# A decode block on one core: part of the query weights' load moves to ScalarE's DMA queue, ahead of x

## The chip, the cores and the metric

The kernel runs on one core of one Trainium2 chip. The metric is the device time of one execution in microseconds (us); smaller is better. The engines are called as in the profile: PE (TensorE), DVE (VectorE), ACT (ScalarE), POOL (GpSimd) and SP (SyncE). A transfer is issued by an engine on that engine's own DMA queue; SP's is q1 in the profile, ACT's is q10, and q8 carries the core's own fetches of instructions. All of them are served by the core's 16 DMA engines. Tile sizes are partitions x elements, all float32.

## The reference

One decoding step for two sequences of one token each: layer norm, attention over a cache of 8192 keys for 16 heads of 256, and a bilinear gated feed-forward layer.

```python
def _A_ref(x, k_cache, v_cache, wq, wo):        # B=2, Sq=1, D=448, H=16, Sk=8192, Dh=256
    q = (x @ wq).reshape(B, Sq, H, Dh).transpose(0, 2, 1, 3)
    scores = jnp.einsum("bhqd,bhkd->bhqk", q, k_cache) * (Dh ** -0.5)
    p = _softmax(scores, axis=-1)
    o = jnp.einsum("bhqk,bhkd->bhqd", p, v_cache)
    return o.transpose(0, 2, 1, 3).reshape(B, Sq, H * Dh) @ wo

x = A_x
h = x + _A_ref(_layernorm(x), A_k_cache, A_v_cache, A_wq, A_wo)
g, u = _layernorm(h) @ B_w_gate, _layernorm(h) @ B_w_up
return h + (g * u) @ B_w_down
```

The two caches are 2 x 16 x 8192 x 256 numbers each, 268 MB; the weights are small beside them (wq is 7.3 MB).

## The kernel before, in words

There are 32 pairs of head and sequence (NQ), numbered i. For each, the keys (128x16384, 64 KB in each of 128 partitions) come into one of two buffers `k0` and `k1`, the values (the same size) into the only buffer `v`. DVE makes the scores: it multiplies the keys by the query spread over the partitions (`qb`), L436, and sums over 256, L445, each in a piece of 16 columns of keys and one of 48. ACT makes the exponentials, PE the product with the values (L527).

The work of each engine is written out in one list for each engine (the class `Engine`), and an instruction carries the names of what it waits for; nothing is reordered by a planner. All large transfers are issued by SP, in the order of its list, each with `load` (L176 in the profile):

- `wq`, the query weights, packed as 128x14336. They are put into the value buffer `v`, as `wq_t`.
- the first 16 columns of keys of pair 0 (`k0`, 128x4096), the other 48 (128x12288), then the keys of pair 1 (128x16384). These wait for nothing.
- then, in turn, the keys of pair i+1, which wait for the largest score of pair i-1 (`m`, L458), and the values of pair i, which wait for PE's last product of pair i-1. The values of pair 0 wait for `all_q` instead: PE must have finished the whole projection of the query, since the values overwrite `wq_t`.

At the start, ACT issues the load of `x` (2x448, L259). From it DVE makes the centred x (L312 to L323), PE transposes it (L338), DVE copies it to `xz` (L345) and clears four accumulators in PSUM (L359, whose last one gives the name `set`). PE then waits for `wq`, `xz` and `set` together, and projects the query in eight rounds of 512 columns (L376): 64 matmuls, of which the first 16 give the query of pair 0, which ACT copies and PE and ACT spread to `qb` (L393 to L413). DVE's first score waits for that.

Of the kernel before, what the change touches and what calls it, by code (L numbers as in the profile page):

```python
# [8 lines left out]
B, D, H, SK, DH, F = 2, 448, 16, 8192, 256, 1792  # L9
EPS = 1e-5  # L10
P = 128
# [15 lines left out]
FF = [(n, g) for n in range(4) for g in range(4) if n < FG[g] // P]  # L27
DOWN = (4, 4, 2, 2, 1, 1)
NPART, OPEN_AFTER = 8, 9

LAYOUT = (
    (slice(0, P), slice(0, DC - 1), slice(0, DC - 1)),
# [121 lines left out]
def decode_block(nc, x, k_cache, v_cache, wq, wo, wg, wu, wd, out):  # L154
# [6 lines left out]
    def landing(name):  # L161
        return nc.alloc_semaphore(name=name)
# [4 lines left out]
    V, A, G, S, T = (  # L167
        Engine(nc, *engine)
        for engine in (
            (nc.vector, "dve"), (nc.scalar, "act", ("qsel", "qb"), ("q",)), (nc.gpsimd, "pool"),  # L170
            (nc.sync, "sp"), (nc.tensor, "pe", ("qp", "Q0"), ("heads",)),
        )
    )

    def load(line, dst, src, sem, name, *waits, n=16):
        line.do(lambda: line.e.dma_start(dst, src).then_inc(sem, 16), *waits)  # L176
        known[name] = sem, n
# [59 lines left out]
    wq_t = v_flat[:, : 3 * H * DH + H * DH // 2]  # L237
# [8 lines left out]
    def keys_of(cache, i, lo, hi):  # L246
        h, b = divmod(i, B)
        return cache[b, h].rearrange("(p j) d -> p j d", p=P)[:, lo:hi, :]
# [6 lines left out]
            n=16 * (i // 2 + 1),  # L255
        )

    s_x = landing("x")
    nc.scalar.dma_start(x_sb, x.rearrange("b s d -> (b s) d")).then_inc(s_x, 16)  # L259
    known["x"] = s_x, 16  # L260
    load(S, wq_t, wq, landing("wq"), "wq")
    load(S, k_sb[0][:, :HC], keys_of(k_cache, 0, 0, HC), landing("k0"), "k0")
    load_k(0, lo=HC)
    load_k(1)
# [618 lines left out]
```

## Time and profile before

| | |
|---|---|
| time, median of 3 runs | 1301.42 us (1301.16 to 1301.53) |
| profiled execution: its time, its span | 1300.94 us, 1299.6 us |
| HBM read | 561.19 MB |
| DVE busy | 1132.5 us, 87% of the span |
| PE busy | 471.1 us, 36% |
| DMA, mean busy share of the 16 engines, by queue q1 | 99.8% |
| wq: 7168 KB on SP's queue, from issue to landing | 19.7 us |

The span runs from the first to the last instruction. Windows and timelines count microseconds from the span's start. In the view of the DMA over a short window, the window is cut into 40 equal slices, and a packet (one row of a transfer, in one partition) is counted whole in the slice in which it starts, so a slice can show more than 100% or far more GB/s than the engines can move; such a view tells when rows start. Besides the rows, a queue's packets contain the small completion marks, one for each DMA engine that took part in a transfer.

### The profile page before, as it was taken

How to read it: one execution, taken by the hardware profiler on the slowest of the kernel's cores; microseconds unless marked ns; L12 is line 12 of the kernel's file. 1: busy time of each engine (PE TensorE's matmuls, PEld its weight loads, DVE VectorE, ACT ScalarE, POOL GpSimd, SP SyncE). 2: the span in 40 equal slices, each digit the busy share in tenths (PEclk: the TensorE clock that was granted, in tenths of full speed). 3: DMA queues.
4: the chain of work that ended last, by engine and by line, in shares of the span. 5: the costliest groups of instructions: out<-in, count | busy, mean ns of one | idle time of the engine just before them, and what ended most of it. 6: DMA issues, size and time to landing. Idle time of an engine off the chain costs nothing.

```text
span 1299.6 us, 7381 instructions
## 1 busy us (share of the span) xinstructions
PE 471.1 (36%) x2870; PEld 149.9 (12%) x2870; DVE 1132.5 (87%) x265; ACT 83.5 (6%) x245; POOL 0.8 (0%) x8
## 2 busy tenths in 40 slices
PE   3643214334323433323334322433322343332368
PEld 0111001101001101101101101101100110100113
DVE  1999988889888889888889988889988888988861
ACT  1100000000000000000000000000000000000000
POOL 0000000000000000000000000000000000000000
PEclk9866566666566666556666656666656666655669
DMA  9999999999999999999999999999999999999998
GB/s 412 428 450 422 448 424 444 426 436 436 422 450 422 450 422 448 424 444 426 436 436 422 450 422 450 422 448 424 444 426 436 436 422 450 422 450 422 448 422 365
DMA packets 11382, 561.28 MB, mean 432 GB/s; under 512 B 1394, under 2 KB 1652, under 8 KB 2420
## 3 DMA queue, kind: packets, MB, share of 16 engines
q1 hardware_dynamic: 11376, 561.25, 99.8%
q8 instruction: 2, 0.03, 0.0%
q10 hardware_dynamic: 4, 0.00, 0.0%
HBM read 561.19 MB, written 0.06 MB: 432 GB/s over the span
## 4 chain that ended last, share of the span: by engine, by line
DMA 48%; DVE 41%; issue 8%; PE 2%; SPq 0%; DVEq 0%; ACT 0%
DMA k<-in_A_k_cache_dram 45%; DVE s L445 21%; DVE k L436 19%; DMA v<-in_wq_dram 2%; DMA v<-in_wd_dram 1%; PE bank L376 1%; PE bank L561 1%; PE bank L527 1%; DVE m L458 0%; DVE nm L464 0%; DVE rl L469 0%; SPq L176 0%; PE bank L551 0%; DVEq L149 0%; PE bank L367 0%
## 5 line engine op out<-in xcount | busy, mean ns | idle before, releaser
L436 DVE TENSOR_TENSOR k<-k,qb 128x4096 f32<-128x4096 f32 x64 | 555.3, 8676 | 122.6 <-DMA k<-in_A_k_cache_dram 98.9
L445 DVE TENSOR_REDUCE s<-k 128x16 f32<-128x4096 f32 x64 | 555.2, 8675 | 1.1
L527 PE MATMUL bank<-v,p 128*2 128x512 f32 x2048 | 289.5, 729 | 348.0 <-DMA v<-in_A_v_cache_dram 348.0
L527 PEld LDWEIGHTS bank<-v,p 128*2 128x2 f32 x2048 | 53.2, 96 | 577.2 <-DMA v<-in_A_v_cache_dram 370.7
L597 PE MATMUL bank<-nm,row 1*128 1x1 f32 x64 | 18.6, 357 | 230.9 <-DVE nm L464 230.9
L594 PE MATMUL bank<-ident,m 128*1 128x128 f32 x32 | 11.9, 372 | 179.7 <-DVE m L458 179.7
L502 ACT ACTIVATE o_sb<-bank 128x512 f32<-128x512 f32 x32 | 19.1, 597 | 625.9 <-PE bank L527 625.9
L597 PEld LDWEIGHTS bank<-nm,row 1*128 1x128 f32 x64 | 15.9, 306 | 240.3 <-DVE nm L464 240.3
L619 PE MATMUL bank<-sel,o_sb 128*128 128x1 f32 x256 | 33.7, 253 | 22.6 <-ACT o_sb L502 22.6
L367 PE MATMUL bank<-q_sel,ones 2*128 2x256 f32 x68 | 40.2, 691 | 0.0
L619 PEld LDWEIGHTS bank<-sel,o_sb 128*128 128x128 f32 x256 | 31.0, 191 | 52.3 <-ACT o_sb L502 52.3
L376 PE MATMUL bank<-v,xz 128*2 x64 | 30.5, 639 | 16.3 <-DMA v<-in_wq_dram 16.3
L492 ACT ACTIVATE nb<-bank 128x1 f32<-128x1 f32 x32 | 5.5, 171 | 427.0 <-PE bank L597 427.0
L601 PE MATMUL bank<-lsum,ones 128*128 128x1 f32 x64 | 18.7, 361 | 23.5 <-ACT p L494 23.5
L594 PEld LDWEIGHTS bank<-ident,m 128*1 128x1 f32 x32 | 2.5, 79 | 182.7 <-DVE m L458 182.7
L601 PEld LDWEIGHTS bank<-lsum,ones 128*128 128x128 f32 x64 | 16.0, 309 | 26.2 <-ACT p L494 26.2
L404 ACT ACTIVATE q_sel<-q_all,ident 2x256 f32 (+1 forms) x35 | 17.2, 492 | 0.0
L413 ACT ACTIVATE qb<-bank 128x256 f32<-128x256 f32 x34 | 13.0, 383 | 58.2 <-PE bank L367 58.2
L367 PEld LDWEIGHTS bank<-q_sel,ones 2*128 2x128 f32 x68 | 16.4, 297 | 2.2 <-issue 1.7
L494 ACT ACTIVATE p<-s,nb 128x64 f32<-128x64 f32 x32 | 11.1, 348 | 1.0
L504 ACT ACTIVATE oT<-bank,rl 128x2 f32 x32 | 8.4, 262 | 42.0 <-PE bank L619 42.0
L487 DVE COPY k<-bank 128x448 f32<-128x448 f32 x1 | 0.6, 624 | 11.6 <-PE bank L561 11.6
(89 smaller groups left out, 96.0 us busy)
## 6 DMA issues: line engine op xcount, KB each, us to landing
v<-in_wq_dram SPq DMA_DIRECT2D x1, 7168.0 KB, 19.7
k<-in_wo_dram SPq DMA_DIRECT2D x1, 7168.0 KB, 39.6
k<-in_A_k_cache_dram SPq DMA_DIRECT2D x1, 6144.0 KB, 38.1
v<-in_A_v_cache_dram SPq DMA_DIRECT2D x1, 6144.0 KB, 22.8
k<-in_wg_dram SPq DMA_DIRECT2D x1, 3136.0 KB, 27.8
k<-in_A_k_cache_dram SPq DMA_DIRECT2D x1, 2048.0 KB, 24.1
v<-in_A_v_cache_dram SPq DMA_DIRECT2D x1, 2048.0 KB, 27.3
k<-in_wu_dram SPq DMA_DIRECT2D x1, 1792.0 KB, 31.8
```

The source lines that it names most:

```text
L367: lambda *_: nc.tensor.matmul(qb_ps, ones[:B, :], q_sel, start=True, stop=True),
L376: lambda turn, k=k, c=c, xs=xs, base=base: nc.tensor.matmul(q_ps[k], xz[:, xs, :], wq_t[:, bass.ds(turn * QG + base, QG)], start=(c == 0), ...
L404: return nc.scalar.activation(q_sel, q_sb[:, bass.ds(at, DH)], AF.Copy, scale=ident[:B, b : b + 1])
L413: lambda *_: nc.scalar.activation(qb[i % 2], qb_ps, AF.Copy),
L436: lambda *_: nc.vector.tensor_mul(kt, kt, q[:, None, :].to_broadcast([P, hi - lo, DH])),
L445: lambda *_: nc.vector.tensor_reduce(s[:, lo:hi], kt, axis=AX.X, op=ALU.add),
L502: A.do(lambda *_: nc.scalar.activation(o_sb, o_ps, AF.Copy), ("M", i), done=("osb", i))
L527: lambda *_, t=t, g=g: nc.tensor.matmul(o_ps[g : g + 2, :], p_t[:, 2 * t : 2 * t + 2], v_sb[:, 2 * t : 2 * t + 2, :], start=(t < 4), stop= ...
L594: lambda *_: nc.tensor.transpose(mT_ps, m_t, ident), ("m", i), done=("T", i)
L597: lambda *_: nc.tensor.matmul(nb_ps, row, nm, start=True, stop=True),
L601: lambda *_: nc.tensor.matmul(l_ps, ones, lsum, start=True, stop=True),
L619: lambda *_, c=c, k=k: nc.tensor.matmul(oT_ps[:, c : c + 1], o_sb[:, (2 * k + c) * P : (2 * k + c + 1) * P], sel[:, k : k + 1], start=(k = ...
```

## The change

The first 896 of the 14336 columns of `wq_t` (F // 2 = 896, so 3.5 KB of each partition's 56 KB) are loaded by two transfers that ACT issues, ahead of its load of x: one for rows 0 to 87 (EVEN = 88), one for rows 88 to 127. SP loads the other 13440 columns as its first transfer. The three count on one semaphore, and PE waits for 48 instead of 16. Nothing else is changed.

```diff
+EVEN = 88
...
-    s_x = landing("x")
+    s_wq, s_x = landing("wq"), landing("x")
+    for rows in (slice(0, EVEN), slice(EVEN, P)):
+        nc.scalar.dma_start(wq_t[rows, : F // 2], wq[rows, : F // 2]).then_inc(s_wq, 16)
     nc.scalar.dma_start(x_sb, x.rearrange("b s d -> (b s) d")).then_inc(s_x, 16)
     known["x"] = s_x, 16
-    load(S, wq_t, wq, landing("wq"), "wq")
+    load(S, wq_t[:, F // 2 :], wq[:, F // 2 :], s_wq, "wq", n=48)
```

The start of ACT's list before. The first row is the load of x; the last one here is the first instruction that needs DVE's work on x.

```order
L259 DMA x<-in_A_x_dram 2x448 [waits barrier_Pool_Activation_PE_DVE_SP_release]
L90 BRANCH_PREFETCH_HINT
L92 COMPARE_AND_BRANCH
L330 ACT_TABLE_LOAD
L330 ACTIVATE std<-xvar,eps 2x1 [waits dve0]
```

And now (the lines of the changed file are five or one higher):

```order
L263 DMA v<-in_wq_dram 88x896 [waits barrier_Pool_Activation_PE_DVE_SP_release]
L263 DMA v<-in_wq_dram 40x896
L264 DMA x<-in_A_x_dram 2x448
L91 BRANCH_PREFETCH_HINT
L93 COMPARE_AND_BRANCH
L335 ACT_TABLE_LOAD
L335 ACTIVATE std<-xvar,eps 2x1 [waits dve0]
```

The load of x has moved from the first to the third place of ACT's queue; its 2 rows stand behind 128 rows of 3.5 KB.

The start of SP's list before:

```order
L176 DMA v<-in_wq_dram 128x14336
L176 DMA k<-in_A_k_cache_dram 128x4096
L176 DMA k<-in_A_k_cache_dram 128x12288
L176 DMA k<-in_A_k_cache_dram 128x16384
L90 BRANCH_PREFETCH_HINT
L92 COMPARE_AND_BRANCH
L176 DMA v<-in_A_v_cache_dram 128x16384
```

And now:

```order
L177 DMA v<-in_wq_dram 128x13440
L177 DMA k<-in_A_k_cache_dram 128x4096
L177 DMA k<-in_A_k_cache_dram 128x12288
L177 DMA k<-in_A_k_cache_dram 128x16384
L91 BRANCH_PREFETCH_HINT
L93 COMPARE_AND_BRANCH
L177 DMA v<-in_A_v_cache_dram 128x16384
```

SP's order is the same; only the width of its first transfer has changed. The last row is the load of the values of pair 0, the one that waits for the whole projection.

## The prediction, made before the changed kernel was run

> **What bounds the kernel now.** I read the slices of the page first, then its DMA queues, then the chain that ended last, and at the end short windows of the DMA at the two places that the change touches.
>
> ```profile
> PE 471.1 (36%) x2870; PEld 149.9 (12%) x2870; DVE 1132.5 (87%) x265; ACT 83.5 (6%) x245; POOL 0.8 (0%) x8
> DMA  9999999999999999999999999999999999999998
> q1 hardware_dynamic: 11376, 561.25, 99.8%
> q8 instruction: 2, 0.03, 0.0%
> HBM read 561.19 MB, written 0.06 MB: 432 GB/s over the span
> ```
>
> The DMA is full in every slice; DVE, the busiest engine, has 87%. So the kernel ends when its 561 MB have come. 432 GB/s over 16 engines is 27.0 bytes a nanosecond for each engine, the figure I use below: a row of 64 KB takes 2.43 us, one of wq's 56 KB 2.12, one of the 13440 columns left 1.99, one of k0's 16 KB 0.61, one of 3.5 KB 0.13. Only three things can move the end: bytes, a time in which the DMA engines have nothing to do, and unevenness among them. The change moves no byte more or less.
>
> The place where the queue could run dry is the load of the values of pair 0. In the chain that ended last, in order of time, and in the timeline (start, duration, engine; ACTq and SPq are issues of transfers):
>
> ```profile
> 0.74 19.69 DMA v<-in_wq_dram
> ```
>
> ```profile
> 0.73 0.54 ACTq L259 DMA_DIRECT2D x<-in_A_x_dram  x1
> 0.74 0.38 SPq L176 DMA_DIRECT2D v<-in_wq_dram  x1
> 1.18 1.50 SPq L176 DMA_DIRECT2D k<-in_A_k_cache_dram  x3
> 2.29 0.61 DVE L312 TENSOR_REDUCE xsum<-x 2x1 f32<-2x448 f32 x1 [0.80 <-DMA x<-in_A_x_dram]
> 6.36 1.71 DVE L359 MEMSET bank<- 128x512 f32 x4 [0.16 <-issue]
> 20.76 9.78 PE L376 MATMUL bank<-v,xz 128*2 x16 [16.29 <-DMA v<-in_wq_dram]
> 31.10 20.76 PE L376 MATMUL bank<-v,xz 128*2 x48
> 51.89 0.33 SPq L176 DMA_DIRECT2D v<-in_A_v_cache_dram  x1
> 66.70 0.33 SPq L176 DMA_DIRECT2D k<-in_A_k_cache_dram  x1
> ```
>
> x is there at 2.29 and everything that PE needs of it at 6.36 + 1.71 = 8.07; PE waits on for wq until 20.76 (wq lands at 20.43, by the chain's row) and then needs 31.13 us until SP may issue the values, at 51.89. When did the engines come to those values? The window 57.6 to 59.2, in slices of 0.04 us, shows when their rows start (1638 GB/s is one row of 64 KB):
>
> ```profile
> GB/s 0 0 0 0 0 0 0 0 1638 0 1639 4915 1638 3277 4916 0 1638 3277 0 0 0 1638 0 0 0 0 0 0 1638 0 0 0 0 0 0 0 0 0 0 0
> DMA packets 32, 1.05 MB, mean 655 GB/s; under 512 B 16, under 2 KB 16, under 8 KB 16
> ```
>
> Sixteen rows, one for each engine: the first at 57.94, most by 58.3, the last at 58.74, just as each engine ends its keys. An issue takes 1.0 us until rows flow (next fence), so the values were ready at 52.9: a margin of 5.0 us. The keys of pair 2, issued at 66.70, have one of 19.4 us of values (8 rows of 2.43) in front of them, a margin of 9.6 us. So the projection may start up to 5 us later than 20.76 at no cost, and every microsecond beyond is one in which the DMA stands still, which nothing later gives back, since the queue is full from there to the end.
>
> The start of the transfers, 1.5 to 2.5 in slices of 0.025 us (2294 GB/s is one row of 56 KB):
>
> ```profile
> GB/s 0 0 0 0 0 0 143 0 0 4588 6881 0 2294 4588 4588 0 4588 0 0 4588 0 0 0 0 0 0 0 0 0 0 2294 0 0 0 0 0 0 2294 0 0
> q1 hardware_dynamic: 16, 0.92, 280.8%
> q10 hardware_dynamic: 4, 0.00, 2.6%
> ```
>
> x's packets start at 1.65, wq's between 1.73 and 2.44, 1.0 us after SP's issue at the earliest. x has 4 packets, two rows and two marks, so its 2 rows are on two engines; the 128 rows of wq are on 16, eight each.
>
> **The change, part by part.**
>
> *The shares of the engines.* Both rows above are equal shares, so I take equal shares on as many engines as allow them: 88 rows on 11 engines with 8 each, 40 rows on 10 with 4 each. If both start with the same engine, ten engines carry 12 rows of 3.5 KB instead of 8 (+14,336 bytes, +0.53 us), one 8 as before (0), five none (-28,672 bytes, -1.06 us). [...] What the shift is worth is seen where the transfers end, in 1290 to 1298 (slices of 0.2 us, 27 GB/s is one engine):
>
> ```profile
> GB/s 394 466 430 430 394 394 502 394 430 376 394 341 448 448 412 394 448 358 466 394 403 385 385 403 403 412 367 197 90 72 54 45 54 54 9 0 0 0 0 0
> ```
>
> Most engines are done at 1295.5; two go on alone until 1296.8. The end waits for these two. If they are among the five relieved, the end comes up to 1.06 us sooner, but no engine of the ten may become the last, so some 0.7; if among the ten, 0.53 later. That is -0.7 to +0.5, and I take 0, since nothing shows which engines they are. And where the queue runs dry, below, all engines start again together, and this shift is gone.
>
> *ACT.* It issues three transfers instead of one, 0.54 us each, so x's issue ends 1.1 us later; ACT's next work waits for x's variance anyhow. The two table loads lie beside that wait. Cost nothing by itself: cover is x's own lateness.
>
> *x behind the rows of wq.* This is the term that counts. On x's two engines ACT's queue holds 8 rows, a mark, 4 rows, a mark, then x: x's is turn 15 of that queue, and SP's queue beside it is full. How an engine shares its time between two queues is shown only by the instruction fetches of q8, one of them in 77 to 79:
>
> ```profile
> q1 hardware_dynamic: 32, 1.05, 123.0%
> q8 instruction: 1, 0.02, 2.9%
> ```
>
> Its 16 KB packet took 2.9% of 16 x 2 us, 0.93 us. Alone it would take 0.61, and with the bytes split evenly between it and a row of 64 KB 1.2; it is nearer to having gone through whole. So I take turns of one row each: a row of ACT's, a row of SP's. ACT's rows begin some 0.09 us before SP's (1.65 against 1.74), so n of ACT's turns go ahead before SP's first row, and 15 - n of SP's turns lie in front of x. Its first eight are rows of 1.99 us, the ninth is a mark, the others are k0's rows of 0.61. Bounds for n: 1, which is what 0.09 us allow at the pace of 0.13 us a row, and 8, the whole first transfer, if the engine asks for rows ahead of their data. I take 4, because ahead is asked (a full queue flows without gaps, 99.8%) but the lead is less than one row's time. Then x's data come at 1.65 + 12 x 0.13 + 8 x 1.99 + 2 x 0.61 + 0.1 for x and marks + 0.6 for the slow first row = 21.1, and DVE sees them 0.3 later, 21.4. (The 0.6: 8 rows of 2.12 after 1.74 would have ended wq at 18.7, it was seen at 20.43, so 0.4 to 1.4 less the 0.3 of being seen; ten of the sixteen engines being early, as in the window at 58, I take 0.6.) n = 1 gives 23.2, n = 8 18.1.
>
> *What then is late.* DVE's chain from x to the last memset is 8.07 - 2.29 = 5.78; PE follows 0.05 later, at 27.2 instead of 20.76, 6.5 late. The wq rows themselves have come by then, so that wait ends first. Behind PE hang ACT's copies and DVE's first score, late by as much; DVE has room to catch up, since one of the 32 pairs costs it 35.4 us (1132.5 / 32) and the DMA 38.8 (2 x 19.4). SP's issue of the values comes at 51.89 + 6.5 = 58.4, rows flow at 59.4. The engines would have begun them at about 58.2, so 1.2 us are lost, and 0.6 for a slow first row again (0 at least, 1.1 at most): **+1.8 us**. The keys of pair 2 come to 66.70 + 6.5 = 73.2, ahead of need: the values end at 59.4 + 19.4 = 78.8, and the issue takes 1.0. For n = 1 the values' rows flow at 61.2, +3.0 and the 0.6, +3.6; for n = 8 at 56.1, inside the margin, 0.
>
> Sum: 1.8 on the profiled 1300.94 is 1302.7; the median of the runs is 0.48 above that execution, so **1303.2**, 0.14% more. A measurement of this kernel can tell about 0.2% (2.6 us) from no change, so I call it the same.
>
> **Rivals.**
>
> *x is early enough* (26%). n is 8, or x's two engines carry few of the new rows, or the engines share by less than a row. For it: ACT's queue has its rows at 1.65 and SP's come later. Against: the q8 packet was nearer to going whole, and 0.09 us is less than one row. Then only the unevenness acts: 1300.7 to 1301.9.
>
> *x comes last of all* (19%, the other side). n is 1 or 2, as the pace of rows in 0.09 us says. Every k0 row ahead of x costs 0.61 in the stall. It decides where x is seen after 22.2, since 2.6 us are lost then: 1304.0 to 1305.3, slower.
>
> *Turns of a whole transfer* (8%). An engine ends the eight rows and the mark of one queue's transfer before it takes the other queue: ACT's 8 rows, wq's 8 (15.9 us), ACT's 4, k0's 8 (4.9 us), then x: 1.65 + 1.6 + 15.9 + 4.9 + 0.1 + 0.6 + 0.3 = 25.1, 3.7 later than my 21.4, so 1306.9. The q8 packet speaks against it if it fell within a transfer, which this view doesn't say. [...]
>
> *Changing the queue costs time* (9%). The q8 packet took 0.3 us more than its bytes, and the two engines late at the end are 1.2 late, which the two q8 packets of the page could have made: 1.2 - 0.6 for their bytes leaves 0.6 a change and back. Fourteen such turns would be 8.4 us on x's engines; x at 29.8, the values' rows at 67.8 instead of 58.2, with the 0.6 of the restart 10.2 more: 1311.6. Against it: x's own packets ahead of wq left wq's first rows all started by 2.44.
>
> *A gain above 0.2%* (2%): the most that can be had is the two late engines' 1.3 us.
>
> **How the numbers follow.** Forecast 36%, the rivals 26, 19, 8, 9 and 2. Same: 36 + 26 less a little for the forecast's upper edge (n = 3 gives 1303.8 and the 1.1 of a slow restart lifts it over 1304.0): 0.58. Slower: 19 + 8 + 9 and that edge: 0.40. Faster 0.02. The range takes in the forecast and the first two rivals, 81%: 1300.7 to 1305.3. The forecast's own is 1301.9 to 1304.3.
>
> **What would show it.** Right: x seen by DVE at 20.5 to 22.5; PE's first L376 at 26.3 to 28.3, released by DVE and not by wq; SP's issue of the values at 57.4 to 59.4; a gap before their rows, which all start together. Wrong: x before 19.5, and PE again released by wq at about 21 (first rival); wq landing later than 21.5 (turns of transfers, or a cost of change). If the values' rows start without a gap and the time moves still, the unevenness of the engines is what I have undervalued, and the last two engines at the end will show it.

## The result, and the profile after

The changed kernel takes 1308.91 us by the median of all its six executions, against 1301.3 before; the ratio is 1.0055, 95% interval [1.0044, 1.0066]. One of the six took 1498.82 us, and seven executions of four experiments below (g1, e1, g3, h1) took 1458 to 1499; no trace of such an execution was taken, and the comparisons leave them out. The other five took 1307.07 to 1309.61, where the kernel before stays within 1301.16 to 1301.53. The profiled execution took 1307.07, 6.1 more than that of before; it is the fastest of the five, and the other four have no trace. So the change makes the kernel slower by 0.55%; 1303.2 had been forecast, and the range ended at 1305.3.

From the page of the changed kernel:

```profile
DMA  9999999999999999999999999999999999999998
q1 hardware_dynamic: 11376, 560.79, 99.7%
q10 hardware_dynamic: 153, 0.46, 0.1%
HBM read 561.19 MB, written 0.06 MB: 430 GB/s over the span
```

The same bytes, 0.46 MB of them now on ACT's queue. The slices of the page show the DMA as full as before, and would let one think that nothing happened; a packet's time counts as busy however slowly its bytes come (in 27 to 57 below, 101.3% with 391 GB/s, and before 100.8% with 437). The timeline of the changed kernel's start shows what did (ACTq, DVE, PE and SPq rows; L numbers are five or one higher than before):

```profile
0.73 0.96 ACTq L263 DMA_DIRECT2D v<-in_wq_dram  x2
1.72 0.27 ACTq L264 DMA_DIRECT2D x<-in_A_x_dram  x1
25.89 0.61 DVE L317 TENSOR_REDUCE xsum<-x 2x1 f32<-2x448 f32 x1 [24.39 <-DMA x<-in_A_x_dram]
29.96 1.71 DVE L364 MEMSET bank<- 128x512 f32 x4 [0.16 <-issue]
32.18 8.37 PE L381 MATMUL bank<-v,xz 128*2 x16 [4.12 <-DVE bank L364]
41.11 20.76 PE L381 MATMUL bank<-v,xz 128*2 x48
61.90 0.33 SPq L177 DMA_DIRECT2D v<-in_A_v_cache_dram  x1
```

x is seen at 25.89 instead of 2.29, PE is now released by DVE's memset and not by wq, and the values of pair 0 are issued at 61.90 instead of 51.89: the path of the forecast, 3.5 us later than forecast. And a second thing, which was not forecast: rows are slow. The DMA of before and then of the changed kernel in the windows 4 to 18 (wq) and 27 to 57 (keys of pairs 0 and 1), two lines or one for each:

```profile
DMA packets 112, 6.42 MB, mean 459 GB/s; under 512 B 0, under 2 KB 0, under 8 KB 0
DMA packets 240, 13.11 MB, mean 437 GB/s; under 512 B 16, under 2 KB 16, under 8 KB 16
```

```profile
DMA packets 167, 5.67 MB, mean 405 GB/s; under 512 B 0, under 2 KB 0, under 8 KB 66
q1 hardware_dynamic: 101, 5.43, 96.2%
q10 hardware_dynamic: 66, 0.24, 4.4%
DMA packets 233, 11.73 MB, mean 391 GB/s; under 512 B 24, under 2 KB 24, under 8 KB 24
```

Rows are counted where they start, so GB/s over a short window is a rough measure: in 4 to 18 an engine starts six or seven rows, and one more or less is 14%. The busy shares are better: a share, times 16 engines and the length of the window, divided by the packets, is the mean time of a packet. The window 47 to 57, in which only 64 KB rows start, before and then now:

```profile
q1 hardware_dynamic: 64, 4.19, 96.7%
```

```profile
q1 hardware_dynamic: 55, 3.60, 93.3%
```

That is 2.42 us for a 64 KB row before and 2.71 now, 12% more, though ACT's queue is empty by then and the transfers are those of the kernel before. In 4 to 18 a wq row of 52.5 KB takes 2.13 us (96.2% over 101 packets), where the same row takes 1.99 in e4 below (98.4% over 111): 7% more.

The trace also keeps the start and the duration of every packet; times of single rows below that no view shows are read there. Before, the engines end the keys of pair 1 between 57.95 and 58.75, 58.2 on the mean; now between 63.13 and 65.16, 64.4 on the mean. The changed kernel in 57 to 67, in slices of 0.25 us (262 GB/s is one row of 64 KB):

```profile
GB/s 1835 0 524 262 524 0 0 0 262 524 524 1573 0 524 262 524 0 0 0 262 524 786 1311 0 524 262 524 0 0 262 262 786 1573 0 0 0 262 786 262 262
q1 hardware_dynamic: 77, 4.00, 100.4%
```

The values, issued at 61.90, can flow from about 62.9, before the first engine has done with its keys, and each engine goes straight on from keys to values (the first five take 2.7 to 3.4 us for their first row of values, the other eleven 2.42). So the gap of the forecast is not in this execution: no engine waited, and the keys alone, ending 6.2 us late, account for the 6.1 us. Two questions follow: what the late x costs where rows are not slow, and what starts the slow rows.

### The profile page after: what moved, and what is told of

Read it like the earlier page. It is cut to its first block, busy times and chain, and to the rows that moved or that the text cites. A ratio compares the mean times of both kernels' runs of the same rounds, so it can differ in the third digit from the quotient of the medians.

```text
span 1305.7 us, 7383 instructions
## 1 busy us (share of the span) xinstructions
PE 472.3 (36%) x2870; PEld 150.1 (11%) x2870; DVE 1132.4 (87%) x265; ACT 83.4 (6%) x245; POOL 0.8 (0%) x8
## 4 chain that ended last, share of the span: by engine, by line
DMA 74%; PE 25%; DVE 0%; issue 0%; SPq 0%; ACTq 0%; ACT 0%
DMA v<-in_A_v_cache_dram 71%; PE bank L532 23%; PE bank L381 2%; DMA x<-in_A_x_dram 2%; DMA v<-in_wd_dram 1%; SPq L177 0%; DVE bank L364 0%; ACTq L263 0%; PE bank L372 0%; DVE xvar L332 0%; DVE xsum L317 0%; DVE o_sb L330 0%; DVE xc L324 0%; PE bank L810 0%; DVE xz L350 0%
## 5 line engine op out<-in xcount | busy, mean ns | idle before, releaser
L418 ACT ACTIVATE qb<-bank 128x256 f32<-128x256 f32 x34 | 13.0, 383 | 58.2 <-PE bank L372 58.2
## 6 DMA issues: line engine op xcount, KB each, us to landing
v<-in_A_v_cache_dram SPq DMA_DIRECT2D x1, 6144.0 KB, 21.4
```

Of the source, the lines that this page charges most:

```text
L418: lambda *_: nc.scalar.activation(qb[i % 2], qb_ps, AF.Copy),
```

## Experiments

Every kernel is compared with the kernel before in the same session (medians 1301.16 to 1301.40). "Values" are those of pair 0.

**e1: x first on ACT's queue.** The first of three undoings: x no longer behind other rows, the two transfers kept.

```diff
     s_wq, s_x = landing("wq"), landing("x")
+    nc.scalar.dma_start(x_sb, x...).then_inc(s_x, 16)
     for rows in (slice(0, EVEN), slice(EVEN, P)):
         nc.scalar.dma_start(wq_t[rows, : F // 2], ...).then_inc(s_wq, 16)
-    nc.scalar.dma_start(x_sb, x...).then_inc(s_x, 16)
```

> Both ACT transfers stay, but x is issued ahead of them. Late-x theory (the loss is the values of pair 0 being issued 10 us late): x seen at 2.3 us, PE starts with wq at about 21, values issued at about 52, time 1301.3 +- 0.6. Slow-rows theory (two queues taking turns slow the rows of all engines, 24 instead of 27 bytes a ns, from the start to the values of pair 0): rows of the keys of pairs 0 and 1 still take 2.03 and 2.7 us instead of 1.82 and 2.42, the keys of pair 1 end near 62 instead of 58, time 1305 or more.

Two executions are compared, 1302.46 and 1310.51, too few and too far apart for a ratio. In the profiled one (1310.51) x is seen at 3.1 us, but now wq itself is late, and with it the values:

```profile
27.24 9.55 PE L381 MATMUL bank<-v,xz 128*2 x16 [21.92 <-DMA v<-in_wq_dram]
58.14 0.33 SPq L177 DMA_DIRECT2D v<-in_A_v_cache_dram  x1
```

The window 27 to 57 has this:

```profile
DMA packets 234, 11.58 MB, mean 386 GB/s; under 512 B 26, under 2 KB 26, under 8 KB 26
```

The engines end their keys between 64.29 and 66.75, long after the values were issued, so none waited for them: the slow rows make this loss (9.6 us) alone. They don't come from the late x. The late-x theory alone is refuted by this run.

**e2: only x late.** The kernel before, with x behind the first keys on SP's queue.

```diff
-    nc.scalar.dma_start(x_sb, x...).then_inc(s_x, 16)
     load(S, wq_t, wq, landing("wq"), "wq")
     load(S, k_sb[0][:, :HC], keys_of(k_cache, 0, 0, HC), landing("k0"), "k0")
+    load(S, x_sb, x..., s_x, "x")
```

> The kernel before, with x issued by SP behind the first 16 columns of the keys, so that x is late and nothing else is changed; one queue, no small rows. This prices lateness by itself. Late-x theory: x seen at about 25, PE at 31, values issued at 62 and flowing at 63 instead of 58.2: a gap of 4.5 us in which no engine moves anything, time 1306 +- 0.7. Slow-rows theory: rows at the full pace of 27 bytes a ns up to that gap. If the rows are slow here too, lateness of the projection is what slows them.

1306.86 us, ratio 1.0045 [1.0028, 1.0062]. x is seen at 25.01. The window 57 to 67 of this run, in slices of 0.25 us (262 GB/s is one row of 64 KB):

```profile
GB/s 0 0 0 0 0 0 0 0 0 0 0 0 0 0 0 0 0 0 0 0 0 0 786 2359 524 262 262 0 0 0 0 0 0 0 0 2359 1573 262 0 0
```

The first values start at 62.5; nothing starts for 5.5 us. Rows run at 437 GB/s in 27 to 57, as before, and the engines end their keys between 57.98 and 58.65, as before. Lateness by itself, with no row slowed, costs 5.7 us: about as much as the changed kernel lost, but by waiting.

**e3 and f1: the same three transfers on one queue.** In e3 SP issues the 88 and the 40 rows ahead of the wide transfer, in f1 behind it; x is alone on ACT's queue.

```diff
-    for rows in (slice(0, EVEN), slice(EVEN, P)):
-        nc.scalar.dma_start(wq_t[rows, : F // 2], ...).then_inc(s_wq, 16)
+    for rows in (slice(0, EVEN), slice(EVEN, P)):          # e3; in f1 behind the next line
+        load(S, wq_t[rows, : F // 2], wq[rows, : F // 2], s_wq, "wq", n=48)
     load(S, wq_t[:, F // 2 :], wq[:, F // 2 :], s_wq, "wq", n=48)
```

> The same three transfers for wq (88 rows, 40 rows, the rest), all on SP's queue in this order, x alone on ACT's queue. Late-x and slow-rows theories: x seen at 2.3, rows at 27 bytes a ns, 1301.3 +- 1.0 (a later start of the five engines without small rows, which carry 1.06 us less). Third theory (the uneven shares of the engines set them apart, and this slows the rows): rows at 24 bytes a ns here too, 1304 or more.

> The uneven transfers (88 and 40 rows) on SP's queue behind the wide one, x alone on ACT's queue: one queue, no turns, but the five engines without small rows run 1.6 us ahead of the ten with them, as in the changed kernel. Offset theory (five engines that far ahead of the rest, however it came about, make all rows slow): rows of the keys of pairs 0 and 1 at 24 bytes a ns, 1305 or much more. Turns theory (only two queues taking turns on uneven engines start the slow pace): 27 bytes a ns, x seen at 2.3, PE at 21.3, and since the two engines that end last were seen among the five without small rows in the run with the small rows first on SP's queue, they end 1 us sooner: 1300.6 +- 0.4.

e3: 1301.7 us, 1.0006 [0.9996, 1.0015]. f1: 1302.76 us, 1.0013 [1.0004, 1.0023], and not the 1300.6 that was expected. In both traces the keys come at full pace (449 and 431 GB/s in 27 to 57). But in f1 the DMA is slow while the small rows move: in the window 18 to 22 the engines are busy 98.8% and bring 254 GB/s.

```profile
DMA packets 199, 1.02 MB, mean 254 GB/s; under 512 B 37, under 2 KB 37, under 8 KB 165
q1 hardware_dynamic: 199, 1.02, 98.8%
```

The small rows take longer than in e4 below (0.21 us on the mean against 0.14), and so do the rows beside them: k0's 16 KB rows that start in 19 to 22 take 1.10 us on the mean, 0.61 from 23 on. There is only one queue with rows of wq here, so a second queue isn't needed for slow rows. wq is complete only at 22.9, 2.2 us later than before. What relieving five engines may bring at the end is more than spent.

**e4: one transfer of 128 rows, still ahead of x.**

```diff
-    for rows in (slice(0, EVEN), slice(EVEN, P)):
-        nc.scalar.dma_start(wq_t[rows, : F // 2], wq[rows, : F // 2]).then_inc(s_wq, 16)
+    nc.scalar.dma_start(wq_t[:, : F // 2], wq[:, : F // 2]).then_inc(s_wq, 16)
...
-    load(S, wq_t[:, F // 2 :], wq[:, F // 2 :], s_wq, "wq", n=48)
+    load(S, wq_t[:, F // 2 :], wq[:, F // 2 :], s_wq, "wq", n=32)
```

> ACT loads the 896 columns in one transfer of 128 rows (8 on each engine, even shares), ahead of x. x is turn 10 of ACT's queue instead of 15: seen at about 20, PE at about 26, values flowing at about 58, so next to no gap. Late-x theory: 1301.5 +- 0.8. Slow-rows theory: turns of two queues slow the rows as in the changed kernel, time 1304 or more. Uneven-shares theory: full pace, 1301.5.

1303.51 us, 1.0017 [1.0007, 1.0026]. In the window 4 to 18 the two queues take turns, as many rows of the one as of the other, and the pace is that of before:

```profile
DMA packets 223, 6.37 MB, mean 455 GB/s; under 512 B 0, under 2 KB 0, under 8 KB 112
q1 hardware_dynamic: 111, 5.97, 98.4%
q10 hardware_dynamic: 112, 0.40, 7.0%
```

x is seen at 21.42 and the values are issued at 57.51; that is later than I expected, and costs 2.3 us. Turns alone don't slow the rows.

**f2: two transfers of 128 rows ahead of x.**

```diff
-    for rows in (slice(0, EVEN), slice(EVEN, P)):
-        nc.scalar.dma_start(wq_t[rows, : F // 2], wq[rows, : F // 2]).then_inc(s_wq, 16)
+    for cols in (slice(0, F // 2), slice(F // 2, F)):
+        nc.scalar.dma_start(wq_t[:, cols], wq[:, cols]).then_inc(s_wq, 16)
...
-    load(S, wq_t[:, F // 2 :], wq[:, F // 2 :], s_wq, "wq", n=48)
+    load(S, wq_t[:, F:], wq[:, F:], s_wq, "wq", n=48)
```

> ACT loads 1792 columns of wq ahead of x in two transfers of 128 rows x 896 each: 18 turns ahead of x instead of 14, but the same share for every engine. Theory that the slow pace needs uneven shares: 27 bytes a ns for wide rows from the keys of pair 0 on; x is seen at about 26, the values are issued at about 63 and flow at 64, a gap of 5.5 us, 1307.5 +- 1. Theory that enough turns suffice, or turns beside the narrow rows of k0: 24 bytes a ns after 25 us here too, little or no gap, a spread of a microsecond or more between runs as in the changed kernel.

1310.45 us, 1.0074 [1.0057, 1.0090]. 437 GB/s in 27 to 57, x seen at 28.61, values issued at 64.75, both later than the 26 and 63 that I expected: more turns make x later still, and the rows stay at full pace.

**f3: x first and one transfer of 128 rows.** Both suspects off, ACT's queue still in use (e1's order with e4's transfer).

> ACT issues x first and then one even transfer of 128 x 896: neither late x nor uneven shares. Both theories: x seen at 2.3, rows at 27 bytes a ns, values issued at about 52: 1301.2 +- 0.4, no difference from the kernel before. If it is slower by over 1 us, turns of two queues have a price of their own.

1301.18 us, 1.0000 [0.9990, 1.0009]. Carrying a part of wq on ACT's queue costs nothing in this form, and brings nothing.

**f4: the uneven split on the gate weights, at the end of the stream, on SP's queue.**

```diff
-    load(S, wg_t, wg, landing("wg"), "wg", ("m", NQ - 1))
+    load(S, wg_t[:, F // 2 :], wg[:, F // 2 :], s_wg, "wg", ("m", NQ - 1), n=48)
+    for rows in (slice(0, 88), slice(88, P)):
+        load(S, wg_t[rows, : F // 2], wg[rows, : F // 2], s_wg, "wg", n=48)
```

> The kernel before, with the uneven split put on the gate weights at the end of the stream, all on SP's queue: the first 896 of their columns as 88 and 40 rows behind the rest. If the two engines that end last are among the five without small rows, they end 1.06 us sooner and the others 0.53 later: 1300.5 +- 0.4. If they are among the ten, 1301.7. With the offset theory the rows after it (up and down weights, 5 MB, 12 us) could be slow, up to 1.4 us more.

1302.53 us, 1.0018 [1.0009, 1.0028]; the ten executions fall into 1301.96 to 1302.60 and 1304.93 to 1305.89, neither of them the 1300.5 or the 1301.7 that I expected. In the profiled one (1301.96) rows beside the small ones are slow again, on one queue: the 14 KB rows take 0.65 us on the mean, 0.54 before. No version of the split was faster than the kernel before.

**g1: the changed kernel again.**

> The changed kernel once more, unaltered, for a second trace of it. If the slow pace begins with the two queues' turns and ends when the early engines stand still for the late values, this trace too shows 24 bytes a ns for the keys of pairs 0 and 1, x seen at 25 to 27, values issued at 61 to 63, and 27 bytes a ns after that; 1307 to 1310. If the slow pace depends on chance, its length and the time differ by a microsecond or more between the two traces, the lateness of x less.

The profiled execution took 1308.26, the two others that are compared 1307.28 and 1310.90; ratio 1.0060 [1.0039, 1.0082]. x is seen at 26.06, the values are issued at 63.51. While wq loads the rows are as slow as in the first trace (405 GB/s in 4 to 18), but then they recover (27 to 57), and the engines stand still (57 to 67, slices of 0.25 us):

```profile
DMA packets 262, 13.42 MB, mean 447 GB/s; under 512 B 26, under 2 KB 26, under 8 KB 26
GB/s 1049 0 0 0 262 262 1311 786 0 262 0 0 0 0 0 0 0 0 0 0 0 0 0 0 0 0 0 0 0 786 2097 786 262 0 262 0 0 0 0 0
```

The last keys start at 59.4, the values not before 64.2. The same kernel loses in two ways: with slow keys and no gap, 1307.07; with fast keys and a gap, 1308.26. Here the rows before 27 us make the keys end 2.4 us later than before (60.6 on the mean), the engines then wait 4.1 us on the mean, and the first row of the values takes 3.03 us instead of 2.42.

**g2, g3, g4, h1: other places of the cut.** g2, g4 and h1 are e1 (x first) with EVEN = 96, 120 and 64, g3 is the changed kernel with EVEN = 96. One number differs. In h1 the two small transfers have equal numbers of rows, 64 and 64, each for one half of the partitions; which partitions an engine writes no trace shows.

> x first, then the two ACT transfers with 96 and 32 rows instead of 88 and 40: the same bytes, rows and turns in all, but 6 + 2 rows on each of the 16 engines. Against the run with x first and 88 rows it differs by one number. Theory that uneven shares on two queues start the slow pace: 27 bytes a ns throughout, 1301.2 +- 0.5, all runs alike. Theory that two transfers beside SP's are enough: rows at 23 to 24 bytes a ns after 8 us, 1303 or more, single runs far longer.

> The change itself with 96 and 32 rows instead of 88 and 40, ahead of x: even shares, x is turn 11 of its queue instead of 15. Uneven-shares theory: full pace, only the lateness is left: x seen at 22 to 23, values issued at 58 to 59, 1303.5 to 1304.5. Otherwise slow rows and 1306 or more.

> x first, 120 and 8 rows: 15 engines with 8 rows, 8 of them with one more, one engine with none. A small dose of unevenness. If the slow pace needs a group of engines that runs ahead by 1 to 2 us, full pace and 1301.2 +- 0.5; if any uneven share on a second queue starts it, rows below 25 bytes a ns in the first 60 us, and runs that differ by microseconds.

> [...] Theory that the slow pace is started by an engine writing partitions that another engine is writing at that time: rows below 26 bytes a ns while wq loads, 1302 or more, runs that differ by microseconds. Theory that only uneven numbers of rows (an engine being done earlier) start it, for which 6 + 2 rows count as uneven: full pace, 1301.2 +- 0.4.

| | cut | median us of the compared executions | ratio, interval | profiled execution, us | us of a 52.5 KB row in 4:18, of a 64 KB row in 47:57 |
|---|---|---|---|---|---|
| f3, x first | none, 128 rows | 1301.18 | 1.0000 [0.9990, 1.0009] | 1301.08 | 1.99, 2.42 |
| h1, x first | 64 and 64 | 1303.30 | 1.0018 [1.0007, 1.0028] | 1303.06 | 2.13, 2.42 |
| g2, x first | 96 and 32 | 1303.08 | 1.0021 [1.0008, 1.0034] | 1313.05 | 2.12, 2.92 |
| g4, x first | 120 and 8 | 1302.62 | 1.0011 [1.0001, 1.0020] | 1303.01 | 2.20, 2.42 |
| g3, x third | 96 and 32 | 1305.83 | 1.0047 [1.0024, 1.0071] | 1306.02 | 2.21, 2.42 |

The profiled execution of g2 is the longest of its ten. The lines of h1 for 4 to 18 (the 16 packets under 512 B are the marks of its first small transfer, so 16 engines took part in it):

```profile
DMA packets 189, 5.64 MB, mean 403 GB/s; under 512 B 16, under 2 KB 16, under 8 KB 89
q1 hardware_dynamic: 100, 5.38, 95.3%
```

Equal numbers of rows don't help: the uneven-shares theory falls with h1, and with g2 if its 96 and 32 rows are shared as equally (6 and 2 on each engine, an estimate). What the runs with slow rows have, and f3, e4 and f2 don't, is a transfer of part of the 128 partitions beside a transfer of all of them: on the second queue in the changed kernel, e1, g1 to g4 and h1, on SP's own in f1 and f4. (The two rows of x are such a transfer too, in every run; they take 1.1 us at most. e3 has its small rows ahead of the wide ones on SP's queue; its wq rows took 2.02 us, hardly more than 1.99.)

After the small rows have gone, rows stay slow in the traces of the changed kernel, e1 and g2 (2.71, 2.79 and 2.92 us for a 64 KB row in 47 to 57), and are back at 2.42 in those of g1, g3, g4 and h1. The slow pace ends within the rows that are under way at an event: in the changed kernel when the first engines start on the values just issued (63.1), in e1 and g2 when q8 fetches instructions (83.92 and 82.10). That is three coincidences; no run tests whether the event is the cause.

## Why the prediction was wrong

*The mechanism was right in part.* x behind ACT's rows, turns of single rows, PE released by DVE, the values issued late: all of it is in the traces, and e2 shows that this path alone costs 5.7 us. The last link, the DMA without work, is in the traces of g1 and e2 and not in the first one of the changed kernel, in which slow rows made the loss. For a time that moves without a gap the forecast had named the unevenness of the engines; what the trace shows is slow rows on all 16 (no 64 KB row that starts in 45 to 62 takes under 2.60 us). So the forecast's test for the cause (PE released by DVE and not by wq) came out as said; its numbers and its gap did not.

*The step that failed* is the term "x behind the rows of wq", and in it above all the price of a row, taken as 27 bytes a ns for every row whatever runs beside it. It gave x seen at 21.4 and the values issued at 58.4; measured are 25.89 and 61.90 (26.06 and 63.51 in g1). By its terms:

- *x seen at 21.4, measured 25.89.* n, ACT's turns ahead of SP's first row, was taken as 4, an estimate from the 99.8%; that rows are asked for ahead of their data no run shows. The window 1.5 to 4 of the changed kernel has 16 rows of SP's, one for each engine, and 22 of ACT's, two for each of 11:

```profile
q1 hardware_dynamic: 16, 0.86, 90.5%
q10 hardware_dynamic: 22, 0.08, 21.9%
```

On one of x's two engines the packets of the trace are in this order: two of ACT's rows, then a row of SP's and a row of ACT's in turn, with the marks as turns of their own, and x behind SP's eight wq rows, its mark and four of k0's. So n was 2, the lower side of my range, and the turns were as forecast; in 4 to 18 above, too, 66 rows of ACT's on 11 engines are 6 each, and SP's 101 are 6 on each of those and 7 on each of the five others. On this engine the 4.5 us are:

| term | taken, us | measured, us |
|---|---|---|
| start of ACT's first row | 1.65 | 2.14 |
| SP's eight wq rows, the first one slow | 16.5 | 17.4 |
| k0 rows in front of x | 2 x 0.61 | 4, together 3.29 |
| ACT's 12 small rows | 1.56 | 1.84 |
| from the end of x's data to DVE | 0.3 | 1.25 |

n = 2 makes 1.2 of them (two more k0 rows of 0.61). Rows slower than 27 bytes a ns make 2.0: 0.85 on the wq rows, 0.85 on the k0 rows, 0.3 on ACT's own. x's completion mark makes 0.95: it is a turn of its own behind one more of k0's rows (x's data end at 24.64, the later mark starts at 25.30). I had counted the marks of the two transfers before it and not this one. The rest is the later start.

- *x to PE:* 5.83 taken, 6.29 measured (25.89 to 32.18): PE followed the memset by 0.5 us, not 0.05.
- *PE's projection:* 31.13 taken, 29.72 measured; its first 16 matmuls took 8.37 us instead of 9.78. In g1 it was 31.15.

*From the issue to the time.* Each profiled time less 1300.94, beside the issue of the values:

| | e4 | g3 | e2 | changed | g1 | f2 |
|---|---|---|---|---|---|---|
| values issued at, us | 57.51 | 60.65 | 61.76 | 61.90 | 63.51 | 64.75 |
| profiled time less 1300.94, us | 1.86 | 5.08 | 5.78 | 6.13 | 7.32 | 8.87 |
| issue less loss | 55.65 | 55.57 | 55.98 | 55.77 | 56.19 | 55.88 |
| engines end the keys of pair 1, mean, us | 58.3 | 60.2 | 58.2 | 64.4 | 60.6 | 58.4 |
| then wait for the values, mean, us | 0.5 | 1.6 | 4.8 | 0 | 4.1 | 7.5 |

In these six traces each microsecond of lateness beyond 55.8 costs one. In five of them the engines wait, and slow rows before the wait only shorten it; that is the forecast's mechanism. The forecast's sum had 56.6 in place of 55.8 (rows wanted at 58.2, less 1.0 for the issue, less 0.6 for the restart; the margin of 5.0 given before it counts to the first row, at 57.94). The restart was right: where the engines waited, the first row of the values took 3.0 to 3.1 us instead of 2.42. In e2 the values' rows began 1.2 us after the issue on the mean, not 1.0; the rest of the 0.8 stays open.

The changed kernel's first trace lies on this line without a wait. Its slow rows lasted until the values came, so that the keys ended about when values issued at 61.90 could flow. Whether that is chance, or the coming of the values ended the slow pace, stays open. Lateness alone doesn't set the time: e1 and g2 are far off the line (values issued at 58.14 and 55.13, 9.57 and 12.11 us lost, no engine waiting). So each of the two, late values and slow rows, is enough for a loss of this size. Which of them made the untraced executions slower, 1307.28 to 1310.90, isn't shown.

*The even-share estimate* (11 engines with 8 rows, 10 with 4) is borne out by the 22 and 66 rows, and by the 153 packets of q10: they are 130 rows and 23 marks, and the trace has 11 of these at 18.33 to 18.79, 10 at 23.55 to 24.10 and x's 2 at 25.21 and 25.30. That x's engines are among those with 12 small rows no row of before showed; on the engine followed above there are 12 ahead of x. What the shift of shares would bring at the end was put at 0; nothing in the runs says otherwise, and f4 and f1, made to collect it, lost 1.4 and 1.6 us.

*The rivals.* "x comes last of all" had the right n and ended at 1305.3, since it knew neither the slow rows nor x's own mark. "Turns of a whole transfer" gave 1306.9, near the result by luck, and is refuted: the 66 rows show turns of single rows. Its sign, wq landing later than 21.5, came all the same (wq's last small row ended at 23.3), so that sign could not tell it from the forecast. "Changing the queue costs time" is refuted by e4: 112 turns, 455 GB/s.

*What starts the slow rows* is only bounded. In these runs they came with a transfer of part of the partitions beside one of all of them, on either queue (a 52.5 KB row of wq took 2.12 to 2.21 us in the changed kernel, g2, g3, g4 and h1; f1 brought 254 GB/s in 18 to 22), and not with one of 128 rows (1.99 us in f3 and e4). What such a transfer does to the others was not shown. h1 was chosen for the theory that an engine then writes partitions that another engine is writing; its 2.13 against 1.99 us agrees, but no trace shows which partitions an engine writes. Why the rows stay slow after the small rows are gone, in some executions and not in others, stays open: no run isolates it.

## What to carry to other kernels

Before a transfer is put ahead of another on a queue, count the rows ahead of the second and multiply by the rows of the *other* queue, since here an engine alternated row by row, 3.5 KB against 52.5 KB and 16 KB: x stood behind 14 turns of its own queue, and so behind eight 52.5 KB rows, a mark and four 16 KB rows of the other. Count the small load's own completion mark as one more turn (part of 0.95 us here), and don't take the price of a row as fixed when a second transfer runs beside it (2.13 us for a 52.5 KB row, 1.99 in e4). A small load from which a chain of work starts belongs first in its queue (x was seen at 25.89 behind the rows, at 3.1 in e1). And if a load must be split over two queues, split it by columns with all 128 partitions in each part (f3: no cost, 1.0000), not by partitions (h1, g2, g4: 0.1 to 0.2%, and 1313.05 us in one execution of g2).

## What the runs showed of the hardware that was not expected

Rows of the same transfers, the same bytes from the same places, ran 12% slower for tens of microseconds (2.71 instead of 2.42 us for a 64 KB row in the changed kernel, 2.79 in e1 and 2.92 in g2, there until about 80 us) with the DMA shown as full all the while, and then were back at 2.42 within one row or two. The busy share didn't show it. GB/s over a long window did (391 against 437 in 27 to 57), and so did the busy share multiplied out to the time of one row.
